# Sixty-four-key blocks, packed sinks and one transposes buffer in an attention ahead of routed experts

## The chip, the cores and the metric

One core of a Trainium2 chip. The metric is the device time of one execution in microseconds (us). The clock granted to the matrix engine (PE) differs from run to run too, but not in step with the time. A run counts as slow when it is over 1.5% above the fastest run of the same kernel, otherwise as fast. Kernels submitted together ran on one chip, with runs of the kernel before between them. The chips differ: the kernel before took about 224 us on one and 214 on two others, so a time is only compared with that of the kernel before in the same rounds.

The engines are PE, VectorE (DVE), ScalarE (ACT), GpSimd (POOL) and SyncE (SP), which here only issues transfers.

## The reference

```python
# attention: 4 sequences, 8 heads, 768 positions, 64 wide
scores = scale * q @ k.T
keep = causal                                    # heads 0, 2, 6: "full"
keep = causal & ((key < 4) | (query - key < 64)) # heads 1, 3, 4, 5, 7: "banded", 4 sinks
x = softmax(where(keep, scores, -1e9)) @ v       # -> 3072 tokens x 512
# experts: 8, chosen by a given domain id for each token
out[mask_e] = relu(x[mask_e] @ w1[e]) @ w2[e]    # w1: 512x1024, w2: 1024x512
```

## The kernel before

Heads are worked on in pairs, four pairs a sequence, 16 in all, numbered 0 to 15: (0,2) full-full, (6,7) mixed, (1,3) and (4,5) banded. For each pair q and k are loaded by SP, cast to half precision on POOL, transposed on PE into PSUM, evacuated to qT and kT, and multiplied in rounds of 1024 score columns; ScalarE takes the exponential of a round; PE multiplies by v and a column of ones; VectorE divides. Scores live in three buffers of 4 KB a partition (`ps_s`), transposes and value products share two of 2 KB (`ps_b`). The transposes of the next pair and the value products of the last one are issued between the score rounds:

```python
ps_s = ctx.enter_context(tc.tile_pool(name="ps_s", bufs=3, space=PSUM))
ps_b = ctx.enter_context(tc.tile_pool(name="ps_b", bufs=2, space=PSUM))
...
# t_items: q and k each get their own PSUM tile
cell["ps"] = ps_b.tile([P, 8, P], FP16, tag="b", name=f"tp{nm}_{n}")
...
evac = nc.scalar.copy if n == 0 and nm == "q" else nc.vector.tensor_copy
...
for n in range(NPAIR + 1):
    hooks(n)                       # loads, casts; stores and weight loads at some n
    ...
    if R == 3:                     # banded pair: 3 rounds
        steps = [T["q"] + A, T["k"] + B_]
    else:
        steps = [T["q"] + A, T["k"] + B_[:h], B_[h:]]
    for x, step in enumerate(steps):
        scores(n, range(2 * x, min(2 * x + 2, R)))
        if n >= 1 and route:
            route.pop(0)()         # one of 20 routing items, on VectorE
        run(step)
```

The routing items work out, from the domain ids, which token goes to which slot of which expert (`map_i`). When a sequence is done its rows are stored to `x_tok` in device memory. At n = 14 GpSimd zeroes the slot tiles and gathers tokens of the first three sequences from `x_tok` by `map_i`; the experts start on those.

```python
ws = {6: (0, 1), 12: (1, 1), 13: (2, 1)}   # hooks(n): loads of expert weights, 1 MB each
if n == 14:
    for u in range(4):
        ...
        nc.gpsimd.memset(xe_t[u][:, 0:2, :], 0.0)
    for pr, g in ((0, 0), (0, 1), (0, 3), (0, 4), (1, 0), (1, 1)):
        load_xe(pr, g, 3)                  # the gathers
    load_w(3, 1)
```

The softmax here doesn't subtract the row's maximum and nothing guards it: scores larger than these inputs give would overflow.

## Time and profile before

| | before |
|---|---|
| median of 3 runs | 223.31 us (223.19 to 224.22) |
| profiled run | span 225.8 us, clock 0.951, slow |
| first exponential of pairs 0, 4, 8, 12, 14 | 9.2, 32.8, 52.7, 73.0, 83.4 us |
| store of sequence 2 (counted from 0), first gather | 77.8, 87.3 us |
| first matmul of an expert | 97.8 us |

In the table by stage a line gives the window, then the busy time of each engine with its number of instructions, the granted clock (1.00 is full), the DMA share and GB/s. The clock column does not show the slow start: it reads 1.00 there, although six transposes take 0.82 us at 11.8 us and 0.51 us from 15.3 us on. Below, the time of PE's first rise is read from such durations, and falls from the clock column. In the waits view a line gives who waited for whom, the total in us, how often, and the longest. In the timeline a line gives start, duration, engine, line, operation, tiles and, in brackets, how long the engine was idle ahead of it and what it waited for.

### The profile page before, as it was taken

The page shows a single profiled execution, that of the slowest core. Times are in us where ns is not written, and L with a number is a line of the kernel's source. Part 1 is how long each engine was busy: PE and PEld are TensorE (multiplying, and loading weights), DVE is VectorE, ACT ScalarE, POOL GpSimd, SP SyncE. Part 2 cuts the span into 40 slices and gives each one's busy share as a digit, 9 for nine tenths or more (in the row PEclk, how much of TensorE's full clock was granted, in tenths as well). Part 3 has the DMA queues.
Part 4 walks back from the last instruction along what each step waited for, and adds up shares of the span by engine and source line. Part 5 has one row for each costly group of instructions (what it writes and reads, how often), then busy time and mean ns, then how long its engine had stood idle before and what let it go on. Part 6 is the DMA issues. An engine that isn't in the chain of part 4 may idle for free. (4 is left out here: it accounts for less than half of the span.)

```text
span 225.8 us, 4791 instructions
## 1 busy us (share of the span) xinstructions
PE 187.7 (83%) x1959; PEld 123.0 (54%) x1959; DVE 98.7 (44%) x200; ACT 92.1 (41%) x120; POOL 120.7 (53%) x170
## 2 busy tenths in 40 slices
PE   0888779989899999289969499999999999998430
PEld 0455455656576675169958495455554564443210
DVE  1448999998977574142110105520244002433210
ACT  2487248855775885115634260025400461000000
POOL 2446768774666884740178743657566403027611
PEclk9999999999999999859997999999999999999955
DMA  6999999999999998399649999996999999704321
GB/s 190 325 298 312 288 299 298 328 291 281 280 343 320 216 249 172 107 170 235 167 90 212 207 256 209 256 219 185 183 185 280 214 220 279 201 17 168 131 93 48
DMA packets 42909, 49.79 MB, mean 220 GB/s; under 512 B 27263, under 2 KB 35712, under 8 KB 42882
## 3 DMA queue, kind: packets, MB, share of 16 engines
q0 software_dynamic: 7936, 26.75, 52.9%
q1 hardware_dynamic: 34802, 22.62, 35.2%
q8 instruction: 17, 0.28, 0.5%
q10 hardware_dynamic: 144, 0.07, 0.2%
q14 instruction: 10, 0.08, 0.1%
HBM read 56.76 MB, written 10.49 MB: 298 GB/s over the span
## 5 line engine op out<-in xcount | busy, mean ns | idle before, releaser
L343 ACT ACTIVATE eT<-sp 128x1024 f16<-128x1024 f32 (+2 forms) x68 | 57.4, 919 | 28.5 <-PE sp L306 26.0
L718 ACT ACTIVATE hT<-h 128x512 f16<-128x512 f32 (+2 forms) x48 | 32.1, 668 | 62.5 <-PE h L711 61.3
L711 PE MATMUL h<-xT,w 128*128 128x256 f16 (+2 forms) x384 | 53.6, 302 | 0.4 <-issue 0.4
L727 POOL DMA_INDIRECT out_dram<-oute,out_i x27 | 27.0, 1001 | 38.7 <-DVE oute L725 33.0
L711 PEld LDWEIGHTS <-w 128*128 128x128 f16 x384 | 40.6, 117 | 11.5 <-issue 0.6
L761 PE MATMUL o<-w,hT 128*128 128x512 f16 x184 | 41.9, 379 | 0.0
L725 DVE COPY oute<-o 128x512 f32<-128x512 f32 x23 | 15.9, 691 | 55.2 <-PE o L761 47.6
L663 POOL DMA_INDIRECT xe<-x_tok,map_i x24 | 24.4, 1019 | 23.7 <-SPq L932 13.1
L396 PE MATMUL av<-ve,eT 128*128 128x65 f16 (+1 forms) x472 | 24.6, 196 | 5.5 <-remote 3.0
L761 PEld LDWEIGHTS <-hT 128*128 128x128 f16 x184 | 17.5, 98 | 19.8 <-issue 0.8
L396 PEld LDWEIGHTS <-eT 128*128 128x128 f16 (+1 forms) x572 | 21.6, 101 | 10.9 <-DVE xb L409 3.9
L306 PE MATMUL sp<-qT,kT 64*128 64x192 f16 (+8 forms) x276 | 23.6, 273 | 2.8 <-DVE kT L292 2.6
L306 PE MATMUL sp<-c16s 128*128 128x128 f16 (+1 forms) x132 | 21.6, 271 | 1.9 <-ACT eT L343 1.7
L158 POOL CAST q<-q 128x768 f16<-128x768 f32 x15 | 12.4, 829 | 15.0 <-DMA q<-in_q_dram 6.4
L178 POOL CAST ve<-v 128x384 f16<-128x384 f32 x32 | 17.0, 558 | 5.5 <-DMA v<-in_v_dram 5.5
L696 DVE COPY xT<-xtp 128x1024 f16<-128x1024 f16 (+1 forms) x16 | 8.8, 552 | 24.0 <-PE xtp L683 24.0
L409 DVE TENSOR_TENSOR xb<-av,rcp 128x384 f16<-128x384 f32 x32 | 17.8, 557 | 1.1
L292 DVE COPY qT<-tpq 128x768 f16<-128x768 f16 x15 | 14.3, 953 | 8.9 <-PE tpq L286 8.9
L158 POOL CAST k<-k 128x768 f16<-128x768 f32 x15 | 13.6, 904 | 7.9 <-PE tpk L286 4.3
L306 PEld LDWEIGHTS <-kT 64*128 64x128 f16 (+1 forms) x276 | 10.8, 96 | 12.4 <-DVE kT L292 4.3
L292 DVE COPY kT<-tpk 128x768 f16<-128x768 f16 x16 | 15.2, 953 | 3.7 <-PE tpk L286 3.7
L753 ACT COPY oute_last<-o_last 128x128 f32<-128x128 f32 x2 | 0.5, 265 | 32.2 <-DVE oute_last L753 32.2
(83 smaller groups left out, 148.4 us busy)
## 6 DMA issues: line engine op xcount, KB each, us to landing
w<-in_moe_w_dram POOLq DMA_DIRECT2D x16, 1024.0 KB
q<-in_q_dram SPq DMA_DIRECT2D x16, 384.0 KB, 5.9
k<-in_k_dram SPq DMA_DIRECT2D x16, 384.0 KB, 6.0
v<-in_v_dram SPq DMA_DIRECT2D x32, 192.0 KB, 5.8
x_tok<-xb SPq DMA_DIRECT2D x4, 768.0 KB, 7.9
out_dram<-oute,out_i POOLq DMA_INDIRECT x27
xe<-x_tok,map_i POOLq DMA_INDIRECT x24
c16s<-c SPq DMA_DIRECT2D x1, 336.5 KB, 5.5
```

Source lines behind the costliest of these rows:

```text
L158: eng.tensor_copy(out=t[:].rearrange("p t h d -> p h t d"), in_=q32_t[nm, n][:])
L178: nc.gpsimd.tensor_copy(out=ve_t[b][:, :, h, 0:D], in_=v_t[b, pi][:, hh])
L292: evac(out=d[:], in_=cell["ps"][:, 0:NSO].rearrange("d t p -> d p t"))
L306: nc.tensor.matmul(out=sp[rows, c : c + w], lhsT=lhsT, rhs=rhs, start=bank not in begun, stop=True, skip_group_check=True,)
L343: nc.scalar.activation(out=eT[n, r // 3][:, r % 3, c0:c1], in_=sp[:, c0:c1], func=AF.Exp, scale=scale)
L396: nc.tensor.matmul(out=ps[m0:m1, it, :], lhsT=eT[n, r // 3][:, r % 3, c : c + w], rhs=rhs, start=(x == 0), stop=(x == len(mms) - 1), skip_ ...
L409: nc.vector.tensor_tensor(out=xb[b][:, :, h * D : (h + 1) * D], in0=ps[:, :, 0:D], in1=rcp[:].unsqueeze(2).to_broadcast([P, NSO, D]), op=A ...
L663: nc.gpsimd.indirect_dma_start(out=xe_of(pr, g), out_offset=None, in_=x_d[0 : 1 + nb * S, :], in_offset=bass.IndirectOffsetOnAxis(ap=map_i ...
L711: nc.tensor.matmul(out=pv[:, a, c0:c1], lhsT=w_t[e, 1][:, c // 2, c % 2, fc * 512 + fr : (fc + 1) * 512 : 4], rhs=xT_t[e][:, c, c0:c1], st ...
L718: nc.scalar.activation(out=hT_t[e][:, 2 * f2 : 2 * f2 + 2, c0:c1], in_=pv[:, :, c0:c1], func=AF.Relu)
L727: inst = nc.gpsimd.indirect_dma_start(out=out, out_offset=bass.IndirectOffsetOnAxis(ap=out_i[:, s : s + 1], axis=0), in_=o[:], in_offset=None,
L761: nc.tensor.matmul(out=ps[:], lhsT=hT_t[e][:, f, g * P : (g + 1) * P], rhs=w_t[e, 2][:, f // 4, f % 4, :], start=(f == 0), stop=(f == 7),)
```

## The change

The intent is less work on PE and ScalarE: banded heads store, for each column of 128 queries, two 64-key blocks in the two halves of the partitions, so that the mask has 768 columns a head instead of more than a thousand; the four sink keys of four row blocks are packed in one 256-column strip; full-full pairs keep six rounds, mixed pairs go from five to four and banded pairs from three to two, so that all rounds come in doubles, seven a sequence instead of ten. The value products need v shifted by 64 keys (`vm`), which VectorE copies, and zeroed sink tiles (`vs`). Transposes of q and k go together into one of the three score buffers; while a banded pair runs, ScalarE evacuates the next pair's q, and VectorE its k.

```diff
-    VS = [[7, 1, 4], [3, 5]]
+    VH, VR = 15, 3
...
+    def copy_vm(n):
+        ...
+        for rows, t0 in ((slice(0, 64), 1), (slice(64, P), 0)):
+            nc.vector.tensor_copy(
+                out=vm_t[b][rows, :, i0 : i0 + 1 + (hB > hA), :],
+                in_=ve_t[b][rows, t0 : t0 + NSO - 1, hA : hB + 1 : st, :],
+            )
...
+        for it in range(NSO):
+            k0 = it * P
+            if it:
+                add(k0, 64, 0, k0, P)
+            add(k0 + 64, 64, 64, k0 + (64 if it else P), P if it else 64)
...
+    def transposes(n, q_evac):
+        ps = ps_s.tile([P, 2, 8, P], FP16, tag="sp", name=f"tp_{n}")
+        ...
+        for x, (nm, store, evac) in enumerate(
+            (("q", qT, q_evac), ("k", kT, nc.vector.tensor_copy))
+        ):
+            d = tpool.tile([P, P, NSO], FP16, tag=f"{nm}T", name=f"{nm}T_{n}")
+            evac(out=d[:], in_=ps[:, x, 0:NSO].rearrange("d t p -> d p t"))
...
+        R = len(plans[n % 4]) // 2 if n < NPAIR else 1
...
+            q_evac = nc.scalar.copy if R == 1 else nc.vector.tensor_copy
+            tr = [lambda n=n, q_evac=q_evac: transposes(n + 1, q_evac)]
+        steps = {1: [tr + av0 + av1], 2: [tr + av0, av1], 3: [tr, av0, av1]}[R]
+        if n < NPAIR:
+            copy_vm(n)
         for x, step in enumerate(steps):
             if n < NPAIR:
-                scores(n, range(2 * x, min(2 * x + 2, R)))
+                scores(n, (2 * x, 2 * x + 1))
             if n >= 1 and route:
                 route.pop(0)()
             run(step)
```

The routing code is unchanged, but it advances one item a step, and there are now seven steps a sequence instead of ten.

## The prediction

> **What bounds the kernel now.** I read the page's busy shares first (PE 83%, DVE 44%, ACT 41%, POOL 53%). They average over two stages with different limits, so I went next to the windows view, which gives each engine's busy time by stretch. Columns: window, us, PE, PEld, DVE, ACT, POOL, clock, DMA share, GB/s.
>
> ```profile
> 30.00:40.00 10.00, 8.58 (x140) 5.76 (x138) 9.86 (x23) 6.59 (x8) 7.40 (x12) 1.00 1.10 297
> 40.00:50.00 10.00, 9.57 (x155) 6.40 (x153) 9.86 (x19) 6.79 (x9) 8.00 (x12) 1.00 1.10 319
> ...
> 80.00:90.00 10.00, 9.89 (x165) 6.59 (x163) 5.72 (x12) 7.10 (x9) 6.09 (x8) 1.00 0.92 222
> 90.00:100.00 10.00, 4.82 (x53) 3.58 (x52) 3.29 (x9) 0.96 (x2) 7.59 (x8) 0.73 0.57 122
> 100.00:110.00 10.00, 10.00 (x99) 9.58 (x98) 1.87 (x4) 5.76 (x10) 0.00 (x0) 0.93 1.04 243
> ```
>
> Attention is the first 92 us, then there is a hole, then the experts. Only attention changes. Inside it no engine is far ahead: from 30 to 50 us VectorE is 98% busy (routing shares it with the evacuations), the DMA engines are above 1.0 of their time, and PE is at 86 to 96%. From 80 us, with routing over, PE alone is at 99%. The page's slices agree (DVE drops from 9s to 5s half way through attention).
>
> The hole at 90 to 100 us decides what a faster attention is worth. The timeline across it (start, duration, instruction, wait):
>
> ```profile
> 77.83 22.87 SPq L420 DMA_DIRECT2D x_tok<-xb  x2
> ...
> 87.31 1.08 POOL L663 DMA_INDIRECT xe<-x_tok,map_i  x1 [3.23 <-DVE xb L409]
> ...
> 91.48 0.74 PE L683 MATMUL xtp<-c16s,xe 128*128 128x128 f16 x8 [1.44 <-issue]
> ```
>
> The third sequence's rows are stored at 77.83 us, the first gather of tokens goes out 9.5 us later, when they have landed, and PE transposes the gathered tokens at 91.48, having already waited 1.44 us. So the start of the experts hangs on the time at which sequence 2 (counted from 0) is finished, not on the time of the last attention pair. The waits view gives the small stalls inside attention:
>
> ```profile
> ACT eT L343 <- PE sp L306: 26.0, 20, 3.4
> ...
> PEld L306 <- DVE kT L292: 4.3, 5, 1.3
> ...
> PEld L396 <- DVE xb L409: 3.9, 9, 0.9
> ```
>
> PE loses some 8 us to VectorE; the exponentials wait for PE, not the reverse. The profiled run is itself a slow one (225.8 us, clock 0.951, against a median of 223.31), so I use it for places and durations only.
>
> **What the Trainium skill says.** (1) "TensorEngine Tiling (Array Packing)", Tiling Modes: a 64x64 tiling is four independent tiles, and changing mode drains the array. The trace agrees on overlap: the 64 half-column matmuls of the half layer (L775, 512 columns) are busy 7.7 us, 1.93 us for each 16, as long as 8 full ones (1.89 us). (2) "VectorE: DVE Perf Modes", zero memsets: one cycle an element, fewer when issued as uint32. The trace agrees: 256 uint32 took 272 ns. (3) "GPSIMD Engine Reference", Key points: it shares its SBUF interfaces with VectorE instructions in a two-port mode or with two SBUF inputs. The trace looks like it:
>
> ```profile
> L538 DVE CAST dest_i<-dst 128x24 int32<-128x24 f32 x1 | 1.3, 1327 | 0.0
> ...
> L547 DVE CAST lof<-lo 128x24 f16<-128x24 int32 x1 | 0.2, 180 | 0.0
> ```
>
> The same 24 elements cost 180 or 1327 ns, and POOL is in its casts 60 to 80% of the time there.
>
> **The change part by part**, per sequence (four pairs of heads; 16 pairs in all). A PE column costs about 0.417 ns at clock 1.00 (four 512-column masks in 1.04 us, less some 0.19 us of latency).
> - Masks. A pair of two banded heads goes from 2176 columns (4x512 + 2x64) to 1536; the mixed pair from 1856 to 1408. Saved: (640+640+448) x 0.417 = 0.7 us.
> - Scores of banded heads. 12+6 matmuls in 0.62+0.56 us become 34 small ones. If the 64x64 and 64x32 tiles overlap, some 30 ns each (the pace of the 24 map matmuls in 0.80 us), so about 1.0 us: no gain, perhaps a little loss from draining.
> - Value products. Both versions have 16 matmuls per banded head; ten of the new ones are half-columns in alternating halves that can run two at a time, five before were half-columns all on one side. Saves about 4 x 33 ns a head, 5 heads: 0.65 us.
> - PE in sum: -1.4 us a sequence, 5 to 6 us in all, plus whatever of the 8 us of stalls goes.
> - ACT: 17 exponential rounds become 14, about 15.6 to 13.3 us a sequence, but 7 of the q evacuations (0.80 us) move to it: about -0.7 us net.
> - VectorE: loses 7 q evacuations of 0.95 us (1.7 us a sequence); gains 24 copies of v into a shifted tile. At 560 ns for a 768-element two-port cast, an estimate is 0.25 us (330 elements) to 0.33 us (660) each when undisturbed, up to twice that beside POOL's casts: 2 to 4 us a sequence. VectorE gets no lighter. Routing (14.1 us, the rest of VectorE's 98.7) advances one item a step, and steps drop from 10 to 7 a sequence: it lasts to the 13th pair instead of the 9th or 10th, so the load moves from sequence 0 into sequences 1 and 2.
> - POOL loses 20 small copies (5.2 us), gets six tiny loads. DMA volume is unchanged. The 12 new memsets at the start (512 uint32 each for six) cost 6 x 0.53 us on VectorE, which is idle until 4.87 us: hidden.
> - Score buffers. There are still three. Before, transposes lived in the other pool; now they take one of the three, so a double round can no longer have its third buffer ready. By hand, at 0.91 us from one exponential to the next, the full-full pair goes from 5.6 us to about 6.1 (ACT stands idle until the next round's masks get a buffer), mixed 4.8 to 4.8, the two banded pairs 4.46 and 3.9 to about 3.6 each (bounded by score, two exponentials, then the q evacuation on ACT). Sum: 18.8 to 18.1 us.
>
> Summed by chain: sequence 0 gains perhaps 2 us (less routing in it), sequence 1 loses most of that to VectorE (11.6 us of evacuations + 3 to 4 of copies + about 8.8 of routing, about 22 to 23 us after the 7% overlap of successive starts, against 20.3 measured), sequence 2 gains 1.5 to 2.5. So sequence 2 ends about 2.5 us earlier. The last sequence gains another 0.7 to 2, but that part ends at the wait for the gather and is lost. Before 223.3 less about 2.7 gives 220.6 us.
>
> **Rivals.**
> 1. VectorE doesn't bind: its 98% was mostly filler and the new copies run at their undisturbed 0.25 to 0.33 us. Then PE's savings and removed stalls come through, sequence 2 ends 6 to 8 us earlier, and the total is 215 to 218 us. For it: PE busy share stays high in the same windows. Against: kT and xb waits of PE on VectorE add to about 8 us.
> 2. Loads bind: DMA share is 1.05 to 1.18 from 6 to 70 us and q, k, v arrive at about one pair per 4 us. Sequences 1 and 2 can't go much below 17 to 18 us each. For it: POOL's casts wait for q in 9 places, 6.4 us. Against: the queue's own waits on POOL show loads held back by buffers. It caps the gain at some 5 us.
> 3. The shared score buffers and the chain of round, exponential, evacuation cost more than I worked out, or small tiles don't overlap (eight 256-column sink matmuls one after the other are 0.85 us a banded pair against 0.2): nothing gained, 223 to 227 us.
> 4. PE waits longer before the gather and its clock falls ("TensorE: Matmul & The Clock Gate", Part 1: an idle window of about 3.4 us brings half clock; here the granted clock was 0.73 in 90 to 100 us): 1 to 2 us given back.
>
> **Range and chances.** Centre 220.6. Rival 1 sets the low end, 216.0; rivals 3 and 4 the high end, 224.5. Faster by over 2% needs 218.8 or less: 0.32. Slower by over 2% needs 227.8: 0.06. Within 2%: 0.62.
>
> **What would show it.** VectorE should still be 90% busy from 25 to 60 us, with the new copies at 0.4 us or more on average; ACT should show a wait for PE in the middle of each full-full pair; banded pairs should repeat every 3.6 us; the store of sequence 2 should go out at about 75 us, and PE's wait for the first gathered tokens should grow from 1.4 to 3 us. If the store goes out before 72 us, rival 1 is right and I am too high; if PE's banded scores take over 1.5 us a pair, rival 3 is.

## The result, and the profile after

The changed kernel is slower: median 236.06 us of four runs (233.98 to 242.37) against 223.76 for the kernel before in the same rounds. The ratio is 1.048, 95% interval 1.036 to 1.059. Ratios here are the mean time of one kernel's fast runs over that of the other's of the same rounds, so not quite the ratio of the medians. The clocks of its five runs are 0.884 to 0.916. Both profiled runs (237.5 us after, 227.6 us before) are slow ones.

The stages in the two profiles, from the first exponential of a pair to that of another, from times rounded to 0.1 us:

| stage | before | after | difference |
|---|---|---|---|
| start to pair 0 | 9.2 | 10.4 | +1.2 |
| pairs 0 to 4 (sequence 0) | 23.6 | 23.0 | -0.6 |
| pairs 4 to 8 (sequence 1) | 19.9 | 25.7 | +5.8 |
| pairs 8 to 12 (sequence 2) | 20.3 | 20.8 | +0.5 |
| pairs 12 to 14 | 10.4 | 15.6 | +5.2 |
| pair 14 to the first expert matmul | 14.4 | 15.7 | +1.3 |
| first expert matmul to the end | 128.0 | 124.5 | -3.5 |

Two stages hold the loss. The table by stage of the changed kernel, for the windows that the prediction showed of before, and finer for the first of them:

```profile
30.00:40.00 10.00, 7.28 (x100) 4.31 (x96) 9.65 (x27) 6.53 (x8) 8.08 (x14) 0.73 1.17 286
40.00:50.00 10.00, 10.00 (x97) 6.15 (x98) 6.23 (x19) 3.66 (x4) 3.21 (x5) 0.50 1.15 327
80.00:90.00 10.00, 7.37 (x89) 4.06 (x90) 9.76 (x19) 6.24 (x8) 7.68 (x11) 0.79 0.99 186
90.00:100.00 10.00, 8.93 (x172) 6.79 (x170) 6.32 (x14) 5.10 (x6) 2.89 (x3) 0.87 0.41 127
100.00:110.00 10.00, 5.72 (x62) 3.37 (x61) 2.80 (x9) 2.05 (x2) 6.84 (x8) 0.65 0.63 131
```

The same view of the changed kernel, cut where its clock falls:

```profile
31.00:35.00 4.00, 1.66 (x20) 1.09 (x21) 3.86 (x11) 1.98 (x3) 4.00 (x8) 0.96 1.12 294
35.00:52.00 17.00, 16.63 (x186) 10.37 (x186) 11.88 (x34) 8.64 (x11) 6.39 (x12) 0.51 1.17 300
```

PE is busy 1.66 of 4 us, the clock falls to one half, and stays there for 17 us although PE is then busy 16.63 of them. Before, the clock was 1.00 in all of these windows up to 90 us.

The traces show when the clock falls, though not what holds it down. Its stretches at one half are one to five times 3.41 us long (3.41, 6.83, 10.24, 13.65 or 17.07 us). The kernels before and after and the eighteen runs below have 25 falls between 30 and 90 us. In the 3.41 us ahead of each, PE was busy for 0.16 to 0.56 of the time. Between them, counted in steps of 3.41 us from each profile's first fall, lie 274 stretches at full clock with no fall after them, and there PE was busy for 0.53 or more. So a stretch in which PE is busy for about half of the time or less comes ahead of every one of these falls.

Why PE was idle is in the waits view of the changed kernel:

```profile
ACT eT L347 <- PE sp L336: 35.8, 28, 2.9
...
PEld L336 <- DVE kT L309: 9.5, 7, 2.1
...
PE sp L336 <- DVE kT L309: 7.8, 7, 1.9
DVE kT L309 <- ACT qT L309: 7.3, 4, 2.4
```

PE's loads of kT wait 9.5 us instead of 4.3, ScalarE's exponentials wait 35.8 us instead of 26.0, and there is a kind of wait that the kernel before did not have: VectorE's evacuation of k waits for ScalarE's of q. This tile is not all of it: in the wait just ahead of the fall (PE idle for 1.90 us until 32.89) the transposes were ready at 29.7 us and q's evacuation ended at 31.4, and k's began at 31.9, behind copies of v and routing instructions on VectorE. One banded pair of sequence 2 at full clock shows the loop, in the timeline of the changed kernel:

```profile
70.45 0.87 PE L336 MATMUL sp<-qT,kT 64*128 64x128 f16 x34
...
71.09 1.94 ACT L347 ACTIVATE eT<-sp 128x1024 f16<-128x1024 f32 x2 [0.57 <-PE sp L336]
...
71.22 0.72 DVE L186 COPY vm<-ve 64x660 f16<-64x660 f16 x2
...
71.59 0.50 PE L300 MATMUL tp<-c16s,k 128*128 128x128 f16 x6
...
71.96 1.29 DVE L578 TENSOR_TENSOR ohl<-c16s,lof 128x512 f16<-128x512 f16 x1
...
72.91 0.81 ACT L309 COPY qT<-tp 128x768 f16<-128x768 f16 x1
...
73.75 0.96 DVE L309 COPY kT<-tp 128x768 f16<-128x768 f16 x1 [0.50 <-ACT qT L309]
...
74.76 0.87 PE L336 MATMUL sp<-qT,kT 64*128 64x128 f16 x34 [0.82 <-DVE kT L309]
```

From one score round to the next it is 0.64 us to the first exponential, 1.94 for two of them, 0.81 for q on ScalarE and 0.96 for k on VectorE: 4.35, measured 4.31. The transposes were ready at 72.1 us; a routing instruction held VectorE until 73.25, and only the last 0.50 us of k's delay is the wait for q. The 34 small score matmuls take 0.87 us, as hoped.

In this sequence, at full clock, the four pairs took 6.65, 5.38, 4.32 and 4.47 us from first exponential to first exponential; before they took 6.30, 5.66, 4.47 and 3.82. So the new layout gains nothing here and loses 0.6 us. In sequence 1 the loss of 5.8 us is in the full-full and the mixed pair, which ran at half clock (7.9 and 9.3 us instead of 5.6 and 5.0), and not in the banded pairs.

At the other stage, the end of routing meets GpSimd's zeroing of the slot tiles, and the store of sequence 2 goes out 12.6 us later than before:

```profile
84.60 3.63 POOL L822 MEMSET xe<- 128x1024 f16 x4
84.82 3.46 DVE L619 TENSOR_SCALAR mb<-mu 128x28 int32<-128x28 int32 x1
...
90.45 0.36 SPq L414 DMA_DIRECT2D x_tok<-xb  x1
...
96.50 1.10 POOL L657 DMA_INDIRECT xe<-x_tok,map_i  x1 [8.26 <-DVE vm L186]
...
106.79 1.02 ACT L347 ACTIVATE eT<-sp 128x1024 f16<-128x1024 f32 x1 [8.63 <-remote]
...
108.62 1.03 PE L677 MATMUL xtp<-c16s,xe 128*128 128x128 f16 x8
```

A multiplication of 28 columns takes 3.46 us. From 98 to 108 us, while the gathers go out, PE gets only some ten instructions every 0.7 us and the last pair's exponentials wait 8.63 us; the kernel before has a shorter stall of the same kind.

### The profile page after: what moved, and what is told of

It is laid out like the page before. It is cut to its first block, busy times and chain, and to the rows that moved or that the text cites. A ratio compares the mean times of both kernels' runs of the same rounds, so it can differ in the third digit from the quotient of the medians.

```text
span 235.7 us, 5092 instructions
## 1 busy us (share of the span) xinstructions
PE 193.3 (82%) x2099; PEld 126.9 (54%) x2099; DVE 108.6 (46%) x229; ACT 90.3 (38%) x115; POOL 117.3 (50%) x152
## 5 line engine op out<-in xcount | busy, mean ns | idle before, releaser
L347 ACT ACTIVATE eT<-sp 128x1024 f16<-128x1024 f32 (+2 forms) x56 | 50.9, 953 | 44.9 <-PE sp L336 35.8
L705 PE MATMUL h<-xT,w 128*128 128x256 f16 (+2 forms) x384 | 52.8, 299 | 0.5 <-DVE xT L690 0.5
L705 PEld LDWEIGHTS <-w 128*128 128x128 f16 x384 | 40.4, 116 | 11.4 <-DVE xT L690 0.7
L336 PE MATMUL sp<-qT,kT 64*64 64x128 f16 (+6 forms) x436 | 30.1, 275 | 11.3 <-DVE kT L309 7.8
L155 POOL CAST q<-q 128x768 f16<-128x768 f32 x15 | 12.4, 827 | 28.9 <-PE tp L300 11.4
L336 PEld LDWEIGHTS <-kT 64*64 64x64 f16 (+2 forms) x436 | 13.0, 107 | 25.2 <-issue 11.5
L386 PEld LDWEIGHTS <-eT 128*128 128x128 f16 (+1 forms) x572 | 20.9, 114 | 7.0 <-issue 6.0
L319 PE MATMUL sp<-c16s 128*128 128x128 f16 (+2 forms) x112 | 19.5, 293 | 6.2 <-ACT eT L347 3.5
L386 PE MATMUL av<-ve,eT 128*128 128x65 f16 (+1 forms) x372 | 22.0, 212 | 0.2
L176 POOL CAST ve<-v 128x384 f16<-128x384 f32 x32 | 16.0, 525 | 6.1 <-DMA v<-in_v_dram 6.1
L309 DVE COPY kT<-tp 128x768 f16<-128x768 f16 x16 | 15.2, 950 | 7.3 <-ACT qT L309 7.3
L319 PEld LDWEIGHTS <-c16s 128*128 128x128 f16 x112 | 9.3, 110 | 12.2 <-issue 6.3
L300 PE MATMUL tp<-c16s,q 128*128 128x128 f16 x96 | 10.0, 254 | 6.4 <-DVE q L155 6.4
```

Source lines behind the costliest of these rows:

```text
L155: eng.tensor_copy(out=t[:].rearrange("p t h d -> p h t d"), in_=q32_t[nm, n][:])
L176: nc.gpsimd.tensor_copy(out=ve_t[b][:, :, h, 0:D], in_=v_t[b, pi][:, hh])
L319: nc.tensor.matmul(out=sp[:, c : c + w], lhsT=id_sb, rhs=c16[:, col : col + w], start=c // 512 not in begun, stop=True, skip_group_check=True,
L336: nc.tensor.matmul(out=sp[o : o + m, c : c + w], lhsT=kT[n][rows, k0 : k0 + m], rhs=qT[n][rows, i0 : i0 + w], start=False, stop=True, skip ...
L347: nc.scalar.activation(out=eT[n, r // 3][:, r % 3, c0:c1], in_=sp[:, c0:c1], func=AF.Exp, scale=scale)
L386: nc.tensor.matmul(out=ps[m0 : m0 + m, it, :], lhsT=eT[n, r // 3][rows, r % 3, c : c + m], rhs=rhs[:, 0 : D + 1], start=(cell["n"] == 1), ...
```

## The experiments

The theory after these views: (a) the shared tile chains k's evacuation behind q's and the exponentials; (b) PE idling on it lets the clock fall; (c) the late routing tail costs the start of sequence 3; (d) the shared score buffer starves the double rounds; (e) in the mixed pair the changes of tile width cost time. Rivals: (f) the loads of q, k and v set the pace; (g) PE's work or VectorE's load is simply too much; (h) the store of sequence 2 lands late because of the weight loads.

| run | this, median (runs) | before, median | ratio of fast runs (95%) |
|---|---|---|---|
| e1_route | 236.4 (4) | 225.2 | too few fast runs |
| e2_order | 235.6 (4) | 225.2 | too few fast runs |
| e3_tp | 234.2 (4) | 225.2 | 1.048 (1.035 to 1.060) |
| e4_warm | 234.7 (4) | 225.2 | 1.055 (1.047 to 1.062) |
| e5_kfirst | 230.1 (4) | 224.3 | too few fast runs |
| e6_nov_after | 234.4 (4) | 224.3 | 1.046 (1.034 to 1.058) |
| e7_nov_before | 226.5 (5) | 224.3 | 1.012 (0.999 to 1.024) |
| e8_w | 235.7 (4) | 224.3 | too few fast runs |
| b1_shared | 217.5 (4) | 214.5 | too few fast runs |
| f1_three | 226.9 (4) | 214.5 | 1.057 (1.049 to 1.064) |
| f2_start | 225.3 (6) | 214.5 | 1.048 (1.042 to 1.054) |
| f3_w | 221.7 (6) | 214.5 | 1.035 (1.028 to 1.041) |
| h0_after | 222.3 (4) | 214.1 | 1.035 (1.028 to 1.042) |
| h1_late | 223.4 (4) | 214.1 | too few fast runs |
| h2_best | 220.0 (4) | 214.1 | 1.021 (1.011 to 1.030) |
| h3_vmpool | 231.0 (4) | 214.1 | 1.076 (1.066 to 1.087) |
| j1_before_w | 220.9 (6) | 224.7 | 0.984 (0.977 to 0.991) |
| j2_kow | 228.0 (6) | 224.7 | 1.004 (0.994 to 1.014) |

Stages of some of the profiles, as in the table above (the chip of f2 and h2 is another one, so only their attention is set beside the others):

| stage | before | after | e1_route | e5_kfirst | f2_start | h2_best |
|---|---|---|---|---|---|---|
| pairs 0 to 4 | 23.6 | 23.0 | 27.7 | 24.9 | 28.6 | 25.9 |
| pairs 4 to 8 | 19.9 | 25.7 | 23.4 | 20.0 | 22.3 | 22.2 |
| pairs 8 to 12 | 20.3 | 20.8 | 21.0 | 20.6 | 19.1 | 21.8 |
| pairs 12 to 14 | 10.4 | 15.6 | 12.0 | 13.4 | 12.0 | 11.7 |

### Routing at the old pace (e1_route)

```diff
-            if n >= 1 and route:
-                route.pop(0)()
+            for _ in range(2 if R < 3 and x == 0 else 1):
+                if n >= 1 and route:
+                    route.pop(0)()
             run(step)
```

> The changed kernel with the routing items popped at the old pace (two a step in the short pairs), nothing else. Theory (the routing tail, pushed to the 13th pair, runs into GpSimd's memsets of the gather tiles): the 3.46 us multiplication is back to about 0.1 us, the last routing instruction ends before 75 us instead of about 89, the store of sequence 2 goes out 2 to 3 us earlier than 90.45 us, and the time falls by 2 to 3 us, to about 233. Rival (VectorE is not on the path there, PE is late by itself because of its clock and its buffers): the collision goes but the time stays within 0.7 us of the changed kernel, or rises because sequences 0 and 1 carry the routing again.

The collision went: the multiplication took 0.18 us at 66.2 us, and pairs 12 to 14 took 12.0 us instead of 15.6. The time did not: 236.4 us. Sequence 0 took 4.7 us more in this profile: the clock rose only at 28 us, and k's evacuation for pair 4 came 3.9 us after its transposes instead of 2.1, behind copies and routing items on VectorE. The store went out at 88.6 us. The rival's second half was right: the load only moved. The 12.0 us still lie 1.6 above the 10.4 before: the full-full pair took 6.5 instead of 5.55 us and the mixed pair 5.5 instead of 4.9.

### The mixed pair in order of width (e2_order)

```diff
+            if retr[PAIRS[n % 4][0]] and not retr[PAIRS[n % 4][1]]:
+                order = la + lb
+            else:
                 ... # interleaved, as it was
```

> The changed kernel with the matmuls of the mixed pair's two double rounds in order 'all 128-wide, then all banded' instead of interleaved. Theory (every change of tile width drains the array[...]): the 20 matmuls of the first mixed double round take 1.0 us instead of 1.69 us at full clock, about 0.7 to 1 us a sequence, and up to 2.5 us of the time. Rival (the exponentials of the mixed pair, four in a row at 0.91 us, are the limit, so a shorter score round is hidden): time within 0.7 us of the changed kernel.

The 20 matmuls took 1.44 us instead of 1.69, not 1.0, and the time stayed (235.6 us). Most of the cost is not in the changes of width between the two lists; the banded list still mixes 128, 64 and 32 columns of weights. Here the rival holds. In this profile, with q still first, sequences 1 and 2 took 20.9 and 20.8 us: the 25.7 us of the changed kernel is one draw.

### Transposes back in the small pool (e3_tp)

```diff
-        ps = ps_s.tile([P, 2, 8, P], FP16, tag="sp", name=f"tp_{n}")
+            ps = ps_b.tile([P, 8, P], FP16, tag="b", name=f"tp{nm}_{n}")  # one for q, one for k
```

> The changed kernel with the q and k transposes back in two separate tiles of the small PSUM pool, so the third score buffer is free for scores and kT does not wait for the evacuation of q. Theory (the shared buffer starves the double rounds of the full-full and the mixed pair): VectorE/ScalarE dependent waits shrink, ScalarE's wait for scores falls from 35.8 us to below 28, the full-full pair falls by 1 us or more, the time by 4 to 6 us to about 231. Rival (what was lost is the clock, from the unchanged pattern of PE idling before kT; or value products now wait for the evacuations of both transposes): the clock still falls to 0.5 inside attention and the time is within 1.5 us of the changed kernel.

234.2 us: less than 2 us against the first median, and its ratio is that of the changed kernel. The clock still fell inside attention (at 37.5 to 40.9 us PE was busy 0.48 of the window). The value products now waited for the evacuations of the transposes, 7.2 us inside 20 to 80 us. The third buffer did count: the full-full pair of sequence 2 took 5.97 us instead of 6.65. But its banded pairs took 5.0 and 4.7 us instead of 4.3 and 4.5. Giving the third score buffer back was not enough.

### Useless work to keep the clock up (e4_warm)

```diff
             sps[r] = sp
+            for _ in range(4 if n and r == 0 else 0):
+                nc.tensor.matmul(out=sp[:, 0:512], lhsT=id_sb,
+                    rhs=c16[:, C_S1 : C_S1 + 512], start=True, stop=True, ...)
             begun = set()
```

> The changed kernel with four useless 512-column matmuls, overwritten by the masks, ahead of the first score round of each pair but the first: 15 x 0.85 us = 13 us of added PE work at full clock, in the place where PE waits for kT. Theory (the half-clock stretches, 17 us from 34.6 us and 7 us from 85.8 us, come from 3.4 us windows in which PE is less than half busy, and cost some 8 us): the clock stays 1.00 from about 20 us to the gathers and the time falls, by 2 to 6 us, in spite of the added work. Rival (the low clock is not from idling, or PE's work at half clock was not on the path): the clock still falls, and the time rises by 5 to 13 us.

All four runs were fast ones, with clocks 0.941 to 0.947 instead of 0.884 to 0.916: idling has a part in the low clock. The time was 234.7 us, with neither the hoped gain nor the loss of 5 to 13 us. In the profile sequence 1 took 23.5 us instead of 25.7, and sequence 2 and pairs 12 to 14 took 21.9 and 18.1 instead of 20.8 and 15.6. A gain from the clock and a cost of the 60 added matmuls may have cancelled. So the run does not show that PE's work is off the path, nor what the clock alone is worth.

### k first (e5_kfirst)

```diff
-        for x, (nm, store, evac) in enumerate(
-            (("q", qT, q_evac), ("k", kT, nc.vector.tensor_copy))
+        for x, nm, store, evac in (
+            (1, "k", kT, nc.vector.tensor_copy), (0, "q", qT, q_evac)
         ):
```

> The changed kernel with k evacuated ahead of q from the shared transposes tile, nothing else. In the changed kernel every banded pair's evacuation of k on VectorE waits for that of q on ScalarE, because both read one PSUM tile, and q's stands behind two exponentials on ScalarE; VectorE, which works in order, stands still meanwhile. Theory (this chain of two exponentials, q, then k sets the pace of the banded pairs): the waits of kT for qT (7 us in four places) go, banded pairs repeat every 3.6 us instead of 4.3, the time falls by 4 to 6 us to about 231. Rival (the pace of the banded pairs is that of the loads of q, k and v, about 4.2 us a pair): pairs still repeat every 4.2 us or more, time within 1.5 us of the changed kernel.

The largest effect of any single edit: 230.1 us (227.3 to 233.4), 5.8 above the kernel before instead of 12.3 for the changed kernel in its rounds. Its two fast runs are 2.0% above the fast runs of the kernel before, against 4.8%. The lowest single runs lie closer together: 227.3 here, 230.9, 230.1 and 229.5 in e1, e2 and e8, and 234.0 in the changed kernel. The waits view of this run:

```profile
ACT eT L347 <- PE sp L336: 24.1, 25, 2.9
ACT qT L309 <- DVE kT L309: 10.9, 6, 6.4
...
PE sp L336 <- ACT qT L309: 6.2, 6, 1.5
...
PEld L336 <- DVE kT L309: 2.7, 4, 0.9
```

The wait of kT for qT is gone, PE's weight loads wait 2.7 us for kT instead of 9.5, and the exponentials 24.1 instead of 35.8. But the tile still ties its two readers, now the other way round: q waits for k, and PE's score matmuls wait 6.2 us for qT where they had waited 7.8 for kT. What differs most is the clock: from its rise at 28 us until after the first gather it never falls. Sequence 1 is back at 20.0 us. One profile is a draw here, too, but others agree: with routing at the slow pace, sequence 1 took 20.9 to 25.7 us and sequence 2 20.8 to 26.0 in the six profiles with q first (after, e2, e4, e6, e8, h0), and 20.0 to 20.4 and 20.1 to 20.6 in the three with k first (e5, h1, j2). Summed over the 16 pairs, the time from the last transpose to the start of k's evacuation was 6.5 us before, 23.8 after and 5.6 here. The banded pairs did not all get to 3.6 us: two of sequence 2 took 4.7 and 4.2, because routing items and copies of v still stand ahead of k on VectorE, and q now waits for k.

### Loads of v left out (e6_nov_after, e7_nov_before)

```diff
         hA, hB = PAIRS[pi]
+        if b:
+            v_t[b, pi] = v_t[0, pi]      # wrong result, on purpose
+            return
```

> Wrong result on purpose: the changed kernel without the loads of v for sequences 1 to 3 (those of sequence 0 are used again), 4.7 MB of the 25 MB moved before the first gather, in small packets. Theory (the loads are nearly the bound in both kernels, and hold the changed one's banded pairs at 4.2 us): the first gather comes 8 us or more earlier than 96.5 us and the time falls by 6 us or more. Rival (the chain of evacuations, exponentials and buffers is the bound, loads are ahead of it): the first gather moves by less than 3 us and the time by less than 2.5 us, apart from the store of sequence 2 landing sooner.

> Wrong result on purpose: the kernel before, without the loads of v for sequences 1 to 3. Theory (loads nearly bound the kernel before, so that a faster attention had little to gain): the time falls by 4 us or more. Rival (VectorE, PE and ScalarE bound it): less than 2 us.

A fifth of the bytes ahead of the first gather was taken away. The changed kernel took 234.4 us, with the first gather at 94.6 instead of 96.5 us, and the kernel before 226.5, not faster at all. The loads bind neither, although the DMA share reads above 1.0 for 70 us. Rival (f) and the prediction's second rival fall.

### Weights issued earlier (e8_w)

```diff
-        ws = {6: (0, 1), 12: (1, 1), 13: (2, 1)}
+        ws = {6: (0, 1), 9: (1, 1), 11: (2, 1)}
```

> The changed kernel with the second and third load of expert weights (1 MB each) issued at the pairs 9 and 11 instead of 12 and 13. In five profiles of the changed kernel and its variants the first gather follows the third of these loads by 12.8 to 13.5 us whatever the time of the store of sequence 2, so the store seems to land only when the weights have. Theory (the store shares the DMA engines with 2 MB of weights): the store lands 3 to 4 us after its issue instead of 4.5 to 11, the first gather comes 2 us or more earlier, the time falls by 1 to 3 us. Rival (the weights only take the place of loads of q, k and v, which now come later): the pairs 10 to 13 are 2 us later each and the time stays within 1 us or rises.

235.7 us, no gain. The first gather came 5.9 us after the issue of the store, against 6.1 in the changed kernel. The constant 13 us in the expectation was a coincidence of the runs it was read from.

### The shared tile alone, in the kernel before (b1_shared)

```diff
-                    cell["ps"] = ps_b.tile([P, 8, P], FP16, tag="b", name=f"tp{nm}_{n}")
+        ps = ps_s.tile([P, 2, 8, P], FP16, tag="sp", name=f"tp_{n}")   # q, then k, as in the change
...
+        q_evac = nc.scalar.copy if R == 3 else nc.vector.tensor_copy
```

> The kernel before with one part of the change alone: transposes of q and k together in one of the three score buffers, q evacuated first and on ScalarE for the banded pairs, k after it on VectorE. All else (ten double rounds, old columns, old sinks, routing pace ten steps a sequence) is as before. Theory (the shared tile makes VectorE's evacuation of k wait for ScalarE's of q behind the exponentials, and takes the third score buffer): VectorE's kT shows waits for ScalarE's qT, banded pairs grow by 0.5 us or more each, the store of sequence 2 goes out 4 us or more after 77.8 us and the time rises by 4 to 8 us above the kernel before of the same rounds. Rival (the loss belongs to the new columns, the small tiles and the copies of v; the buffer is harmless by itself): the time rises by less than 2 us.

The chain appears at once in its waits view:

```profile
DVE kT L290 <- ACT qT L290: 14.4, 7, 3.4
```

But the time rose by only 3.0 us in the medians, with runs from 213.5 to 219.6 of both states, and the two fast runs are at 214.7 us against 214.3 for the fast runs of the kernel before. By fast runs, then, the rival holds, though two are too few to be sure. Nor did the banded pairs grow by 0.5 us each: in sequence 2 they took 4.36 and 4.17 us, against 4.47 and 3.82 before. In sequence 3, where neither kernel has routing left, it was the full-full and the mixed pair that grew, from 5.55 and 4.89 us before to 6.34 and 5.64 (the profile before is from another chip); pair 14 began 3.4 us later than there. The delay of k's evacuation summed to 21.8 us, as in the changed kernel. With three rounds in a banded pair and routing done by 60 us there is more other work to put beside it, and in the profiled run the clock did not fall again after its rise. So the chain by itself is not the whole loss; that it takes the short pairs and the low clock with it is likely, not shown.

### Repairs together (f1_three, f2_start, f3_w)

f1 has k first, the order of width and the old routing pace; f2 moves the zeroing of the sink tiles behind the evacuations of the second pair; f3 also moves a weight load:

```diff
-        ws = {6: (0, 1), 12: (1, 1), 13: (2, 1)}
+        ws = {6: (0, 1), 12: (1, 1)}
...
                 load_xe(pr, g, 3)
+                if (pr, g) == (0, 3):
+                    load_w(2, 1)
```

> The changed kernel with three repairs: k evacuated first, the mixed pair's matmuls in order of width, routing at the old pace. Theory (each takes a different wait off the path to the store of sequence 2): 1 to 3 us faster than with k first alone (230.1 us), store of sequence 2 at 81 us or before. Rival (after k first the bound is elsewhere, in the half clock of the first pairs and the landing of the store): within 1 us of 230.1.

> The same three repairs, and the zeroing of the six sink tiles moved from the start of VectorE's work to after the evacuations of the second pair, their loads one pair later. Theory (the start of the first pair, 1.2 us late, and the late rise of the clock, at 28 us instead of 13 in several runs, cost sequence 0 some 3 to 5 us): first exponential at 9.2 us instead of 10.4, time 2 us or more below the version with three repairs, near the kernel before. Rival (the start is made up for by the loads, which run ahead later): within 1 us of the version with three repairs.

> The same as the version with the moved zeroing, and the third load of expert weights issued after the third gather instead of at pair 13. Theory (the store of sequence 2, issued next to 1 MB of weights, lands 11 us after its issue where it could land in 5): first gather 3 us or more earlier relative to the store, time 1 to 3 us lower, and below the kernel before. Rival (the weights are needed as soon as the gathers, so the wait moves to the third expert): within 1 us.

f1 was a miss: 5.7% above the kernel before, more than the changed kernel had been on any chip. In its profile k's evacuation is 2.5 and 3.0 us late in pairs 3 and 4, behind routing items, and the clock falls twice inside attention. That the old pace undid what k first had given is likely, but no run has just these two. Once routing is over (at 67 us) the layout shows its worth in the banded pairs: 3.5 and 3.4 us in f2, against 4.5 and 3.8 before. The wide pairs give most of it back: in sequence 3 of h2, below, the full-full and the mixed pair take 6.5 and 5.1 us against 5.55 and 4.89 before (on another chip), so that its first three pairs take 15.2 us against 14.9. Moving the zeroing took 0.5 us off the start and 1.6 us off the median, within the spread. Moving the weights gave 3.6 us: the store landed 3.6 us after its issue.

### VectorE's order and load (h0_after, h1_late, h2_best, h3_vmpool)

h1 is k first with copies of v and routing items issued behind each step's evacuations. h2 has this and all of f3, with routing only in full-full and mixed pairs. h3 is h2 with `nc.gpsimd.tensor_copy` for the copies of v.

> The changed kernel again, unaltered, so that the next three can be compared with it on the same chip: 4 to 6% slower than the kernel before, with the evacuation of k late by some 24 us in sum over the 16 pairs.

> k evacuated first, and VectorE's copies of v and routing items placed behind the evacuations of each step instead of ahead of them; pace of routing, sinks, order and weights as in the changed kernel. Theory (what is left is VectorE's order): the delay from the last transpose to the evacuation of k falls from 5.6 us (k first alone) to below 2 us in sum, and the time to 1.5% above the kernel before or less, against 2.6% with k first alone. Rival (VectorE's load is the bound, the order doesn't matter): it stays 2.5% or more above the kernel before.

> All repairs: k first, copies and routing behind the evacuations, routing only in the full-full and mixed pairs (two or three items a step), the mixed pair in order of width, sinks zeroed later, third load of weights after the third gather. Theory (no engine is then held by order): within 1% of the kernel before, or faster by 1 to 2%. Rival (the added VectorE work of the copies and the late landing are structural): 2% or more slower than the kernel before.

> The same with the 24 copies of v on GpSimd instead of VectorE (about 10 us off VectorE). Theory (VectorE's load still binds sequences 0 and 1): 1 to 3 us faster than the version with all repairs. Rival (order was all, and GpSimd's casts, now later, hold the transposes): same within 1 us, or slower.

The changed kernel itself was 3.5% slower on this chip. h1 gave no gain in the median (223.4 against 222.3), though its two fast runs, at 220.5 and 220.7, were faster than all of h0's (whose fast runs are 221.1 to 222.8): two clocks of the same kernel, 0.945 to 0.970 and 0.927 to 0.935, lie 6 us apart. The lateness of k summed to 8.1 us, not below 2. Order alone is therefore not settled by these runs. h2 came to 2.1% above the kernel before, the best of this chip, and not the 1% that theory gave. Two banded pairs at the end of sequence 2 show the pace that the prediction had in mind:

```profile
72.09 0.87 PE L339 MATMUL sp<-qT,kT 64*128 64x128 f16 x34
72.73 1.94 ACT L350 ACTIVATE eT<-sp 128x1024 f16<-128x1024 f32 x2 [0.57 <-PE sp L339]
...
73.78 0.96 DVE L309 COPY kT<-tp 128x768 f16<-128x768 f16 x1 [1.26 <-PE tp L300]
...
74.77 0.80 ACT L309 COPY qT<-tp 128x768 f16<-128x768 f16 x1
...
75.62 0.87 PE L339 MATMUL sp<-qT,kT 64*128 64x128 f16 x34
```

That is 3.5 us a pair, with k's evacuation beside the exponentials and ScalarE alone as the limit. h2 lost time of its own in pair 1, where PE waited 2.15 us for the first routing items, and the clock fell at 25 us. h3 was much slower, for another reason than the one asked about: the last copies of v stood on GpSimd behind the gathers, and PE waited for them.

```profile
111.44 0.22 PE L389 MATMUL av<-vm,eT 128*64 128x65 f16 x1 [15.39 <-POOL vm L186]
```

Its first three stores went out at 45.0, 66.8 and 86.2 us against 43.1, 65.0 and 85.8: taking the copies off VectorE did not speed the attention either. That does not clear VectorE's load, since GpSimd, whose casts the transposes wait for, got the copies instead.

### The weight load, before and after (j1_before_w, j2_kow)

j1 is the kernel before with f3's move of the third weight load. j2 is the changed kernel with k first, the order of width and the same move; routing is left at the slow pace.

> The kernel before with the third load of expert weights (1 MB) issued after the third gather instead of at pair 13. Theory (the store of sequence 2 lands late because it shares the DMA engines with that load, in both kernels): the store lands 4 to 6 us after its issue instead of 8.6, the first gather comes 3 us earlier than 87.3 us, the time falls by 2 to 4 us. Rival (in the kernel before the store goes out just ahead of the load, and the weights are then late for the third expert): within 1 us, or slower.

> The changed kernel with k evacuated first, the mixed pair in order of width and the third load of weights after the third gather; routing, copies and sinks as in the changed kernel. Theory (these three are the waits that cost most, and the routing pace is better left slow): within 1.5% of the kernel before, first gather before 90 us. Rival (what is left is in the attention itself, its late clock in sequence 0 and VectorE's load): 2% or more slower than the kernel before.

j1 is faster than both kernels: 220.9 us, ratio 0.984. Its mechanism is not the one expected. The store still landed after 8.7 us and the first gather went out at 86.9 us. What changed is the stall around the gathers. In the kernel before:

```profile
93.32 0.34 PE L396 MATMUL av<-ve,eT 128*64 128x65 f16 x5
...
95.87 0.20 DVE L408 RECIPROCAL rcp<-av 128x6 f32<-128x6 f32 x1 [4.29 <-remote]
...
96.71 0.51 PE L396 MATMUL av<-ve,eT 128*128 128x65 f16 x6 [3.05 <-remote]
...
97.80 1.47 PE L711 MATMUL h<-xT,w 128*128 128x256 f16 x6
```

and in j1:

```profile
91.88 0.59 PE L396 MATMUL av<-vs,eT 128*128 128x65 f16 x5 [0.18 <-ACT eT L343]
...
92.21 0.93 PE L396 MATMUL av<-ve,eT 128*64 128x65 f16 x11
...
93.71 3.60 PE L711 MATMUL h<-xT,w 128*128 128x256 f16 x16
```

The waits called "remote", in which PE and VectorE stand for 3 and 4 us and the view names no engine as the cause, are under 2 us, and the first expert matmul comes 4.1 us earlier, 0.6 of which was there at pair 14. That the stall comes from the weight load is not shown. It has to do with the chip: the profiles of b1, f1 to f3 and h0 to h3, all from the two other chips, have no "remote" wait at all, and there the changed kernel itself (h0) goes from pair 14 to the first expert matmul in 8.1 us instead of 15.7. j2 has the move and still waits 2.8 and 1.9 us. f3 gained over f2 (6.8 us for this stage instead of 11.4) by the earlier landing of the store. What the stall consists of stays open.

j2 is level with the kernel before in fast runs (1.004), but only two of its six were fast, and its median is 3.3 us above. One of its three repairs, the move of the load, helps the kernel before as well, so the attention is to be judged against j1: the fast runs of j2 are 2.0% above those of j1 (224.9 and 220.5 us). Its first gather went out at 87.2 us, as in j1 (86.9), and its first expert matmul came at 99.3 instead of 93.7. Beside a kernel with the same move the new attention does not break even.

## Why the prediction was wrong

**The step that failed** is "Score buffers", in its last part: the banded pairs "about 3.6 each (bounded by score, two exponentials, then the q evacuation on ACT)". Sequence 2 of the changed kernel, at full clock, took 20.8 us where the hand sum of "Score buffers" said 18.1, and the banded pairs are 1.6 us of the difference. Their chain has one more link. q and k share one PSUM tile, the program makes the second reader wait for the first, and so k's 0.96 us on VectorE comes after q's 0.81 on ScalarE: 4.31 us measured. The prediction noted that the transposes moved to another pool, and did not ask what a common tile does to two readers. The Trainium skill's page "PSUM — Partial Sum Buffer", section "PSUM bank collisions raise a hardware error", says that two engines must not touch the same bank and quadrant at once, reads included, and that software adds a dependency for it. By size the halves are 2 KB a partition each, one bank of that page each, so the rule would allow both at once; the wait that the trace shows (7.3 us in four places) is the program's order for the tile. Where k went first and nothing stood ahead of it, 3.5 us was measured (h2): the sum was right, its chain was not. The same step was too low for the wide pairs: the full-full pair took 6.65 us instead of about 6.1 and the mixed pair 5.38 instead of 4.8. 6.5 and 5.1 us are left in the best repaired run, and b1 shows 6.34 and 5.64 with the shared tile alone. This step explains why the gain did not come; the 12 us of loss are mostly in the next two.

**The second failure** is the size of the clock's term. Rival 4 gave it 1 to 2 us, ahead of the gather. It fell inside attention instead, after windows in which PE stood waiting for kT: sequence 1 took 5.8 us more in this profile, and 20.0 instead of 25.7 us with k first. Where it falls changes from run to run: in h0, the same kernel, the long fall is in sequence 2 (26.0 us), and sequence 1 took 21.0. How much of the 12 us is the clock and how much the waits that bring it about is not separated: e4 raised the clock without gaining time, and b1 had the chain's waits without a fall and lost 3 us in the medians, 0.4 in fast runs.

**The third** is the end of routing. "The load moves from sequence 0 into sequences 1 and 2" was right, and nobody looked at where its tail would land: on GpSimd's zeroing, where one small instruction took 3.46 us. Stage 12 to 14 grew by 5.2 us; e1 took 3.6 of them back and lost as much elsewhere. The other 1.6 us are the slower full-full and mixed pairs.

Point by point:
- That the start of the experts hangs on sequence 2 and not on the last pair was misread. The changed kernel's first gather was 9.2 us late and its end 9.9, but in the kernel before, the changed one and 15 of the other 18 profiles the first expert matmul follows attention's last value products on PE without a gap (in the kernel before at 97.80 us, as the view under j1 shows); in the other three the gap is under 0.5 us. In j1 the gather kept its time and the end came earlier, because PE got through the last pairs. So a gain in the last sequence need not be lost.
- "PE loses some 8 us to VectorE" was read from weight-load lines (PEld); PE's own matmuls waited 2.6 us for kT and 2.1 for xb in that profile.
- PE's terms held where they were measured: 34 small score matmuls 0.87 us (1.0 predicted), half-column value products starting in twos. The mixed pair's score round took 1.69 us, where "a little loss from draining" had been allowed. Its masks go to 1536 columns by the program, not 1408, which is 0.05 us.
- VectorE's copies of v took 0.39 us on average, as estimated. That VectorE gets no lighter was right; that it would be 90% busy from 25 to 60 us was not (6.23 of 10 us from 40 to 50: it waited for a slow PE). Its order of work mattered, which a sum of busy times cannot show.
- The zeroing at the start was called hidden until 4.87 us; it ran to 5.7 us. The first exponential came at 10.4 instead of 9.2 us, and moving the zeroing took back 0.5 of the 1.2 us (f2).
- Rival 3 was the nearest: the chain of round, exponential and evacuation did cost more. Its 223 to 227 us left out what an idle PE does to its clock. Rival 2 fell (e6, e7). Rival 1's premise, that VectorE's load does not bind, is not settled: h3 moved the load to GpSimd without gaining, which speaks for it but does not show it. Its consequence, 215 to 218 us, did not come.
- The store was expected at about 75 us and came at 90.45. That was the sign named for a wrong prediction, in the other direction.

Still open: why h1 gained so little on its chip, the 2% that the best repaired versions stay behind (h2, and j2 against j1), and why the clock stays low while PE is busy.

## What to carry to other kernels

When two things move into one buffer, list who reads it and on which engine: a tile with two readers ties their queues together, and the reader whose queue is longest should come second. An engine's busy time does not tell what a change does to it; write down its order, and ask what stands ahead of the instruction that others wait for. Before taking work off the busiest engine, check what it waits for, because an idle spell may cost its clock as well; and look at large transfers issued next to a latency-bound stage, since moving one of them by 12 us gained 1.6% here (j1), on one chip, while the whole rewrite lost time.

## What the Trainium skill lacked or had wrong

- "TensorE: Matmul & The Clock Gate", Part 1, has half clock after an idle window of about 3.4 us and full clock after about 3.4 us of sustained work. The length fits: stretches at half clock are multiples of 3.41 us here. But the window need not be idle: ahead of the 25 falls between 30 and 90 us PE was busy for 0.16 to 0.56 of it. And the clock stayed at half for 17 us in which the profile has PE busy for 16.63 (it models the ends of matmuls); no run here shows what holds it there.
- "PSUM — Partial Sum Buffer" names the collision of readers in one bank, not the cost in a kernel of a tile that spans two banks and is read by two engines: 7.3 us of waits in the changed kernel, 14.4 in b1_shared.
- "GPSIMD Engine Reference", Key points, gives the shared interfaces, but neither it nor another page says that one VectorE instruction can be held through several GpSimd instructions in a row: a 28-column multiplication took 3.46 us, until the last of four memsets of 0.96 us each had ended (88.28 and 88.23 us), and 0.18 us away from them (e1).
- No page was found on the stall of PE, ScalarE and VectorE while GpSimd issues gathers ("remote" waits of 3.05 and 4.29 us before, 8.63 us after, with the kernel before at about 224 us; none in the profiles of the two chips where it takes 214).
